# Chunked attention and two feed-forward layers: the PSUM scratch of the second layer as one tile of two banks, or as two tiles of one bank

## The chip, the cores and the metric

One core of one Trainium2 chip runs the whole kernel. The metric is the device time of an execution in microseconds (us); the figure for a kernel is the median of its timed runs.

## The reference

Three stages follow each other on 2304 tokens (4 x 576) of 512 features. The first is attention inside chunks of 64 tokens, for 8 heads of 64 features. The other two are feed-forward layers with 2048 hidden features, without residuals:

```python
# layer 1
h = x @ w_in;  g = softplus(h);  x = g @ w_out
# layer 2
h = x @ w_in
P = a[0] + a[1]*h + a[2]*h*h + a[3]*h*h*h
Q = 1 + abs(b[0])*abs(h) + abs(b[1])*h*h
g = P / (Q + 1e-6)
out = g @ w_out
```

The output is float32, 2304 x 512.

## The kernel before

The tokens are cut into five blocks (512, 512, 512, 384 and 384; `BLOCKS`), and the hidden features into 16 slices of 128. A **step** is one slice of one block: 80 steps in layer 1, then 80 in layer 2, numbered on by `s`. In layer 2 the blocks come in the order 512, 384, 384, 512, 512 (`ORDER2`).

A float32 operand is split into two parts, and each product is made of three products of parts. So a step of layer 2 has

- `products_h` (matmuls at L726): 12 matmuls over the tokens of the block into one PSUM bank `h` (pool `ps_h`, two buffers of one bank);
- `rational` (from L779 on), the function above on `h`, by ScalarE (ACT) and VectorE (DVE);
- `products_out2` (L915): three matmuls of 512 columns for each 128 tokens of the block, so 12 or 9, into PSUM tiles `acc` of two banks (pool `ps_acc`, two buffers). They take the upper part of `g` from ACT (L823) and the lower part from GpSimd (POOL, L826).

At the end of a block `evacuate` copies each `acc` tile to SBUF, its first bank by ACT (L948), its second by DVE (L950), and SyncE stores it.

In `rational` a scratch area `u` in PSUM holds one value after the other. In the order in which a step adds them, its operations are:

| engine, line | in the profile | what |
|---|---|---|
| ACT L793 (`square`) | `u<-h` | u = h*h |
| ACT L811 (`linear`) | `t<-h,b_t` | d = abs(b0*h) |
| ACT L841 | `t<-h,na_t` | p = -(a3*h + a2) |
| DVE L796 | `t<-u,absb_t,t` | d = abs(b1)*u + d |
| DVE L852 | `t<-h,t` | p = h*p |
| DVE L796 | `t<-t,na_t,h` | p = (p - a1)*h |
| ACT L815 (`log`) | `u<-t,epsq_t` | u = ln(d + const) |
| ACT L819 (`exp`) | `u<-u` | u = exp(-u), a first reciprocal |
| DVE L796 | `t<-t,epsq_t,u` | d = (d + const)*u |
| DVE L796 | `u<-t,na_t,u` | u = (p - a0)*u |
| DVE L796 | `t<-t,u` | p = (d - 2)*u |
| ACT L823 (`hi`) | `g<-t` | upper part of g |
| POOL L826 (`lo`) | `g<-t,g` | lower part of g |

All DVE operations built by the helper `stt` have L796 as their line; they are told apart by their operands. d and p are SBUF tiles, both named t in the profile.

PSUM is full: `ps_acc` four banks, `ps_h` two, `ps_att` two. `ps_att` holds one tile of [128, 2, 512] float32, used by the attention during layer 1. In layer 2 it is `u`, allocated once in `square` of the first step: even steps use the half [:, 0], odd steps [:, 1].

The order of the work is written out beforehand. `Program` collects every operation as a task with an engine, a cost and the names of what it reads and writes, and `schedule` plans a start for each by its costs; the tasks are then issued in the order of those starts, so each engine works through a fixed list. For the planner the halves of `u` are two things (`ku, kp = ("att", s % 2), turn("t2", 3)`). The waits between engines are not the planner's: the framework below derives them from the tiles which each instruction reads and writes, in the order of issue.

Of the kernel before, what the change touches and what calls it, by code (L numbers as in the profile page):

```python
# [11 lines left out]
F32 = mybir.dt.float32  # L12
# [5 lines left out]
PSUM = bass.MemoryType.PSUM  # L18
DRAM = bass.MemoryType.DRAM

P = 128
# [21 lines left out]
class Program:  # L43
# [24 lines left out]
    def add(self, engine, cost, fn, reads=(), writes=(), alloc=None, after=(), table=None):  # L68


        i = len(self.tasks)
        deps = {}
        before = list(after)
        for key in reads:
            before += [self.writer[key]]
            self.readers.setdefault(key, []).append(i)
        for key in writes:
            if key in self.writer:
                before.append(self.writer[key])
            before += self.readers.pop(key, [])  # L80
            self.writer[key] = i
        for j in before:
            if j != i:
                deps[j] = self.tasks[j][1] + self.delay(self.tasks[j][0], engine)
        if alloc is not None:
            if alloc in self.last_alloc:
                deps.setdefault(self.last_alloc[alloc], 0.0)
            self.last_alloc[alloc] = i
        self.tasks.append((engine, cost, fn))
        self.deps.append(deps)  # L90
        self.table.append(table)
        return i
# [97 lines left out]
def tile_chunk_attention_two_ffn(  # L190
# [43 lines left out]
    dpool = ctx.enter_context(tc.tile_pool(name="dpool", bufs=1, space=DRAM))  # L234
    ps_acc = ctx.enter_context(tc.tile_pool(name="ps_acc", bufs=2, space=PSUM))
    ps_h = ctx.enter_context(tc.tile_pool(name="ps_h", bufs=2, space=PSUM))
    ps_att = ctx.enter_context(tc.tile_pool(name="ps_att", bufs=1, space=PSUM))

    ident = const.tile([P, P], F32, name="ident")
    epsq_t = const.tile([P, 1], F32, name="epsq_t")  # L240
# [12 lines left out]
    def table(name):  # L253

        if loaded[0] != name:
            loaded[0] = name
            act.preload_act_table_set(name)

    def on_act(n, pointers=0):
        return 0.05 + 0.095 * pointers + n / 1200  # L260

    def on_dve(n, pointers=0):
        return 0.07 + 0.06 * pointers + n / 960

    def turn(tag, bufs):

        counts[tag] = counts.get(tag, -1) + 1
        return tag, counts[tag] % bufs
# [6 lines left out]
    x = {}  # L275
# [461 lines left out]
    def scratch(s, n_tok, third=False):  # L737
        t = {}

        def new(tag):  # L740
            if tag == "t1" and third:
                tile = att1.tile([P, T], F32, tag="v", name=f"{tag}_{s}")
            else:
                tile = (tmp if tag == "t1" else tmp3).tile([P, T], F32, tag=tag, name=f"{tag}_{s}")
            t[tag] = tile[:, :n_tok]
            return t[tag]

        return t, new

    def new_g(s, third=False):  # L750
        p, tag = (att1, "qkT") if third else (gpool, "g")
        gs[s] = p.tile([P, 2, T], F32R, tag=tag, name=f"g_{s}")
# [26 lines left out]
    def rational(s, hkey, j, start):  # L779
        n_tok = BLOCKS[j][1]  # L780
        third = s % 3 == 2
        t, new = scratch(s, n_tok, third)
        ku, kp = ("att", s % 2), turn("t2", 3)
        kd, kg = ((("v", 0)), "g third") if third else (turn("t1", 2), turn("g", 2))
        old = [("turned", "later", n) for n in range(16)] if third else []

        def u():
            return x["u"][:, s % 2, :n_tok]

        def square():  # L790
            if start:
                x["u"] = ps_att.tile([P, 2, 512], F32, tag="att", name="u")
            act.activation(u(), h(), AF.Square)  # L793

        def stt(out, in0, scalar, in1, op0, op1):
            return lambda: vec.scalar_tensor_tensor(  # L796
                out=out(), in0=in0(), scalar=scalar, in1=in1(), op0=op0, op1=op1
            )

        def h():  # L800
            return hs[s]

        def d():
            return t["t1"]

        def p():
            return t["t2"]

        def linear():
            table(EXP_LN)  # L810
            act.activation(new("t1"), h(), AF.Abs, scale=b_t[:, 0:1])  # L811

        def log():
            table(EXP_LN)
            act.activation(u(), d(), AF.Ln, bias=epsq_t)  # L815

        def exp():
            table(EXP_LN)
            act.activation(u(), u(), AF.Exp, scale=-1.0)  # L819

        def hi():
            new_g(s, third)
            act.activation(gs[s][:, 0, :n_tok], p(), AF.Copy)  # L823

        def lo():
            pool.tensor_tensor(  # L826
                out=gs[s][:, 1, :n_tok], in0=p(), in1=gs[s][:, 0, :n_tok].bitcast(F32),
                op=ALU.subtract,
            )

        add(
            ACT, on_act(n_tok), square, [hkey], [("att", 0), ("att", 1)] if start else [ku],
            alloc="att" if start else None,
        )
        add(
            ACT, on_act(n_tok, 1), linear, [hkey, "b"], [kd], alloc="v" if third else "t1",
            table=EXP_LN,
        )
        add(
            ACT, on_act(n_tok, 2),  # L840
            lambda: act.activation(  # L841
                new("t2"), h(), AF.Identity, scale=na_t[:, 3:4], bias=na_t[:, 2:3]
            ),
            [hkey, "na"], [kp], alloc="t2",
        )
        add(
            DVE, on_dve(n_tok, 1), stt(d, u, absb_t[:, 1:2], d, ALU.mult, ALU.add),
            [ku, kd, "absb"], [kd],
        )
        add(  # L850
            DVE, on_dve(n_tok),
            lambda: vec.tensor_tensor(out=p(), in0=h(), in1=p(), op=ALU.mult), [hkey, kp], [kp],  # L852
        )
        add(
            DVE, on_dve(n_tok, 1), stt(p, p, na_t[:, 1:2], h, ALU.add, ALU.mult), [hkey, kp], [kp]
        )
        add(ACT, on_act(n_tok, 1), log, [kd], [ku], table=EXP_LN)
        add(ACT, on_act(n_tok), exp, [ku], [ku], table=EXP_LN)
        add(DVE, on_dve(n_tok, 1), stt(d, d, epsq_t, u, ALU.add, ALU.mult), [kd, ku], [kd])
        add(DVE, on_dve(n_tok, 1), stt(u, p, na_t[:, 0:1], u, ALU.add, ALU.mult), [kp, ku], [ku])  # L860
        add(DVE, on_dve(n_tok), stt(p, d, 2.0, u, ALU.subtract, ALU.mult), [ku, kd], [kp])
        add(
            ACT, on_act(n_tok), hi, [kp], [(kg, 0), *old], alloc="qkT" if third else "g"
        )
        add(POOL, 0.2 + n_tok / 430, lo, [kp, (kg, 0)], [(kg, 1)])
        return kg
# [158 lines left out]
    s = -1  # L1025
# [130 lines left out]
```

## Time and profile before

| what | value |
|---|---|
| median of 3 runs | 907.72 us (906.89 to 907.83) |
| profiled execution | 905.86 us, its span 904.1 us |
| mean granted clock of TensorE | 0.997 |
| busy share of the span: PE, PEld, DVE, ACT, POOL | 95%, 80%, 72%, 57%, 29% |
| layer 2 on TensorE | first matmul at 452.97 us; its last 66 matmuls in a row begin at 883.22 us |
| DMA over the span, mean | 79 GB/s |

PE is TensorE's matmuls, PEld its weight loads. A line of the timeline has the start, the duration, the engine, the line of code, the operation with its operands and shapes, and how many alike follow each other; in brackets stands how long the engine was idle before and on whom it waited. The duration of a row runs from start to result, and back-to-back instructions overlap a little, so a pace is read from starts.

### The profile page before, as it was taken

Reading aid. Unit: us, or ns where it says so; the run is one execution under the profiler, and the core shown is the slowest. Engines: PE = TensorE matmul, PEld = TensorE weight load, DVE = VectorE, ACT = ScalarE, POOL = GpSimd, SP = SyncE. Lnnn points to the kernel's source line nnn. Section 1 sums busy time; section 2 is a strip of 40 time slices with the busy share of each in tenths; the row PEclk is TensorE's granted clock in tenths of the full one; section 3 lists DMA queues with packets and bytes.
Section 4 is the critical chain, followed back from the end, with each engine's and each line's share of the span. In section 5 each row is a group of like instructions: output and inputs, shape, how many; then the busy total and the mean of one; then the engine's idle time right before and its main releaser. Section 6 shows DMA issues by size and latency. Waiting matters only on the chain.

```text
span 904.1 us, 13291 instructions
## 1 busy us (share of the span) xinstructions
PE 862.1 (95%) x5068; PEld 726.1 (80%) x5068; DVE 649.2 (72%) x1102; ACT 511.2 (57%) x864; POOL 258.4 (29%) x238
## 2 busy tenths in 40 slices
PE   8999999999999999999989999999898999999977
PEld 7777889999997788888767778788787777778755
DVE  4788787828999888169746677677677776777764
ACT  4899962233334333354477566666766756667653
POOL 0132332221222221253537122421432242212212
PEclk9999999999999999999999999999999999999999
DMA  9784525025444333265412001200000200000001
GB/s 213 200 227 154 187 71 106 12 59 163 117 106 140 105 109 108 70 217 162 129 46 95 0 1 29 100 1 1 36 1 1 82 1 1 0 33 15 1 0 47
DMA packets 76928, 71.11 MB, mean 79 GB/s; under 512 B 36160, under 2 KB 63808, under 8 KB 76864
## 3 DMA queue, kind: packets, MB, share of 16 engines
q1 hardware_dynamic: 76864, 70.27, 27.1%
q8 instruction: 39, 0.64, 0.3%
q14 instruction: 25, 0.20, 0.1%
HBM read 56.63 MB, written 13.63 MB: 78 GB/s over the span
## 4 chain that ended last, share of the span: by engine, by line
DVE 36%; PE 36%; ACT 20%; issue 6%; POOL 1%; DMA 1%; ACTq 0%; DVEq 0%; SPq 0%; POOLq 0%
DVE t L796 18%; PE h L726 16%; PE acc L885 14%; DVE u L796 6%; ACT u L793 5%; ACT u L815 4%; DVE t L852 3%; ACT u L819 3%; ACT t L811 2%; ACT g L823 2%; DVE qkT L520 2%; ACT t L841 2%; PE aps L541 1%; DVE cm_2o L361 1%; DVE cm_2i L361 1%
## 5 line engine op out<-in xcount | busy, mean ns | idle before, releaser
L915 PE MATMUL acc<-w_2o,g 128*128 128x512 f32 x864 | 216.9, 395 | 19.2 <-POOL g L826 11.4
L726 PE MATMUL h<-xT,w_2i 128*128 128x512 f32 (+1 forms) x960 | 212.9, 372 | 11.1 <-DVE t L796 9.5
L726 PE MATMUL h<-xT,w_1i 128*128 128x512 f32 (+1 forms) x960 | 211.3, 370 | 3.1 <-ACT g L766 1.6
L885 PE MATMUL acc<-g,w_1o 128*128 128x512 f32 (+1 forms) x960 | 211.7, 370 | 0.0
L915 PEld LDWEIGHTS acc<-w_2o,g 128*128 128x128 f32 x864 | 159.5, 188 | 64.0 <-POOL g L826 20.9
L726 PEld LDWEIGHTS h<-xT,w_2i 128*128 128x128 f32 x960 | 175.9, 189 | 41.4 <-DVE t L796 14.3
L726 PEld LDWEIGHTS h<-xT,w_1i 128*128 128x128 f32 x960 | 173.6, 188 | 27.5 <-ACT g L766 2.5
L885 PEld LDWEIGHTS acc<-g,w_1o 128*128 128x128 f32 x960 | 173.8, 188 | 23.0
L826 POOL TENSOR_TENSOR g<-t,g 128x512 fp32r<-128x512 f32 (+1 forms) x80 | 94.4, 1180 | 299.9 <-ACT g L823 192.0
L769 POOL TENSOR_TENSOR g<-t,g 128x512 fp32r<-128x512 f32 (+1 forms) x80 | 98.2, 1228 | 238.5 <-ACT g L766 221.7
L761 ACT ACTIVATE t<-h 128x512 f32<-128x512 f32 (+1 forms) x80 | 44.2, 553 | 94.8 <-PE h L726 94.7
L796 DVE SCALAR_TENSOR_TENSOR t<-u,absb_t,t 128x512 f32<-128x512 f32 (+1 forms) x80 | 55.6, 695 | 46.1 <-ACT u L793 22.7
L766 ACT ACTIVATE g<-h 128x512 fp32r<-128x512 f32 (+1 forms) x80 | 44.3, 554 | 63.6 <-PE acc L885 63.0
L520 DVE STREAM_TRANSPOSE qkT<-qk 32x256 f32<-32x256 f32 x176 | 76.9, 437 | 3.0
L796 DVE SCALAR_TENSOR_TENSOR t<-t,epsq_t,u 128x512 f32<-128x512 f32 (+1 forms) x80 | 55.4, 692 | 30.2 <-ACT u L819 25.4
L815 ACT ACTIVATE u<-t,epsq_t 128x512 f32<-128x512 f32 (+1 forms) x80 | 52.0, 650 | 43.3 <-DVE t L796 32.3
L823 ACT ACTIVATE g<-t 128x512 fp32r<-128x512 f32 (+1 forms) x80 | 46.8, 585 | 49.3 <-DVE t L796 47.1
L793 ACT ACTIVATE u<-h 128x512 f32<-128x512 f32 (+1 forms) x80 | 43.2, 540 | 47.3 <-DVE t L796 24.7
L852 DVE TENSOR_TENSOR t<-h,t 128x512 f32<-128x512 f32 (+1 forms) x80 | 50.8, 634 | 24.7 <-ACT t L811 17.8
L796 DVE SCALAR_TENSOR_TENSOR u<-t,na_t,u 128x512 f32<-128x512 f32 (+1 forms) x80 | 55.8, 698 | 10.9 <-ACT u L793 8.1
L796 DVE SCALAR_TENSOR_TENSOR t<-t,na_t,h 128x512 f32<-128x512 f32 (+1 forms) x80 | 55.4, 692 | 8.7 <-ACT u L793 3.7
L796 DVE SCALAR_TENSOR_TENSOR t<-t,u 128x512 f32<-128x512 f32 (+1 forms) x80 | 50.6, 632 | 12.5 <-ACT u L793 6.4
(79 smaller groups left out, 764.0 us busy)
## 6 DMA issues: line engine op xcount, KB each, us to landing
wr_1i<-in_moe_w_in_dram SPq DMA_DIRECT2D x16, 512.0 KB, 3.9
wr_1o<-in_moe_w_out_dram SPq DMA_DIRECT2D x16, 512.0 KB, 4.7
wr_2i<-in_moe_w_in_dram SPq DMA_DIRECT2D x16, 512.0 KB, 3.9
wr_2o<-in_moe_w_out_dram SPq DMA_DIRECT2D x16, 512.0 KB, 4.5
out_dram<-ev SPq DMA_DIRECT2D x18, 256.0 KB, 2.0
qk<-in_q_dram SPq DMA_DIRECT2D x16, 256.0 KB, 5.1
qk<-in_k_dram SPq DMA_DIRECT2D x16, 256.0 KB, 5.3
v<-in_v_dram SPq DMA_DIRECT2D x16, 256.0 KB, 4.6
```

The lines of the kernel that those rows point to most:

```text
L520: vec.transpose(tiles["qkT"][p0 : p0 + 32, n, :, c * CH : (c + 1) * CH].rearrange("p g (u t) -> p g t u", t=2), qk_t[tb][p1 : p1 + 32, h:: ...
L726: pe.matmul(hs[s], w[:, a, c * P : (c + 1) * P], xt[:, b, c, :n_tok], start=n == 0, stop=n == 3 * KC - 1,)
L766: act.activation(gs[s][:, 0, :n_tok], hs[s], AF.Softplus)
L769: pool.tensor_tensor(out=gs[s][:, 1, :n_tok], in0=t["t2"], in1=gs[s][:, 0, :n_tok].bitcast(F32), op=ALU.subtract,)
L793: act.activation(u(), h(), AF.Square)
L796: return lambda: vec.scalar_tensor_tensor(out=out(), in0=in0(), scalar=scalar, in1=in1(), op0=op0, op1=op1)
L815: act.activation(u(), d(), AF.Ln, bias=epsq_t)
L823: act.activation(gs[s][:, 0, :n_tok], p(), AF.Copy)
L826: pool.tensor_tensor(out=gs[s][:, 1, :n_tok], in0=p(), in1=gs[s][:, 0, :n_tok].bitcast(F32), op=ALU.subtract,)
L852: lambda: vec.tensor_tensor(out=p(), in0=h(), in1=p(), op=ALU.mult), [hkey, kp], [kp],
L885: pe.matmul(accs[1, j, half][:, c % 2, :n_tok], wts[1, "o", fc][:, a, c * P : (c + 1) * P], gs[s][:, b, :n_tok], start=first and n == 0, s ...
L915: pe.matmul(accs[2, j, half][:, c % 2], gs[s][:, b, c * P : (c + 1) * P], wts[2, "o", fc][:, a, :], start=first and n == 0, stop=last and ...
```

## The change

The pool `ps_att` goes into an exit stack of its own. In `square` of the first step of layer 2 that pool is closed, a new pool `ps_u` is opened, and two tiles of [128, 512] float32 are allocated in it, one bank each, with tags of their own. Even steps use the one and odd steps the other. Operations, their operands' sizes, the tasks, their costs, names and order stay as they were.

```diff
     ps_h = ctx.enter_context(tc.tile_pool(name="ps_h", bufs=2, space=PSUM))
-    ps_att = ctx.enter_context(tc.tile_pool(name="ps_att", bufs=1, space=PSUM))
+    att_stack = ctx.enter_context(ExitStack())
+    ps_att = att_stack.enter_context(tc.tile_pool(name="ps_att", bufs=1, space=PSUM))
...
         def u():
-            return x["u"][:, s % 2, :n_tok]
+            return x["u", s % 2][:, :n_tok]
 
         def square():
             if start:
-                x["u"] = ps_att.tile([P, 2, 512], F32, tag="att", name="u")
+                att_stack.close()
+                ps_u = ctx.enter_context(tc.tile_pool(name="ps_u", bufs=1, space=PSUM))
+                for n in range(2):
+                    x["u", n] = ps_u.tile([P, 512], F32, tag=f"u{n}", name=f"u{n}")
             act.activation(u(), h(), AF.Square)
```

## Rows read from the trace of the kernel before

**Rows 1.** The page: busy us of each engine, share of span, instructions

```profile
PE 862.1 (95%) x5068; PEld 726.1 (80%) x5068; DVE 649.2 (72%) x1102; ACT 511.2 (57%) x864; POOL 258.4 (29%) x238
```

**Rows 2.** Groups by form, PE, 473.3 to 883.2: busy, mean ns, idle before

```profile
L915 PE MATMUL acc<-w_2o,g 128*128 128x512 f32 x798 | 201.1, 395 | 19.0 <-POOL g L826 11.4 <-ACT g L823 3.8 <-DVE ev L950 3.7
L726 PE MATMUL h<-xT,w_2i 128*128 128x512 f32 x528 | 128.5, 394 | 6.4 <-DVE t L796 6.4
L726 PE MATMUL h<-xT,w_2i 128*128 128x384 f32 x384 | 72.6, 338 | 2.8 <-DVE t L796 2.2 <-ACT u L793 0.5
```

**Rows 3.** Timeline, PE in layer 2: start, us, instruction [idle before, releaser]

```profile
473.31 3.01 PE L915 MATMUL acc<-w_2o,g 128*128 128x512 f32 x12 [1.23 <-DVE ev L950]
...
620.40 4.35 PE L726 MATMUL h<-xT,w_2i 128*128 128x384 f32 x24
624.59 1.08 PE L915 MATMUL acc<-w_2o,g 128*128 128x512 f32 x4
...
788.60 5.60 PE L726 MATMUL h<-xT,w_2i 128*128 128x512 f32 x24
794.04 5.60 PE L915 MATMUL acc<-w_2o,g 128*128 128x512 f32 x24
...
872.70 3.01 PE L726 MATMUL h<-xT,w_2i 128*128 128x512 f32 x12 [1.13 <-DVE t L796]
879.01 4.37 PE L726 MATMUL h<-xT,w_2i 128*128 128x512 f32 x12 [3.30 <-DVE t L796]
883.22 15.93 PE L915 MATMUL acc<-w_2o,g 128*128 128x512 f32 x66
```

**Rows 4.** Chain of waits that ended last, 473.3 to 883.2, by line

```profile
by line: DVE t L796 38.8%; DVE u L796 11.9%; ACT u L793 9.6%; ACT u L815 7.2%; DVE t L852 6.8%; ACT u L819 5.6%; ACT g L823 5.3%; ACT t L811 5.1%; issue 5.0%; ACT t L841 3.2%; DVE ev L950 1.1%; ACT ev L948 0.2%; ACTq L823 0.1%; ACTq L793 0.
```

**Rows 5.** Timeline, ACT and DVE, one step of a 384-token block

```profile
583.21 0.47 ACT L793 ACTIVATE u<-h 128x384 f32<-128x384 f32 x1 [0.21 <-DVE t L852]
...
583.72 0.62 DVE L796 SCALAR_TENSOR_TENSOR u<-t,na_t,u 128x384 f32<-128x384 f32 x1 [0.54 <-ACT u L793]
...
584.38 0.62 DVE L796 SCALAR_TENSOR_TENSOR t<-u,absb_t,t 128x384 f32<-128x384 f32 x1
584.91 0.54 DVE L796 SCALAR_TENSOR_TENSOR t<-t,u 128x384 f32<-128x384 f32 x1
...
585.49 0.58 ACT L815 ACTIVATE u<-t,epsq_t 128x384 f32<-128x384 f32 x1 [1.80 <-DVE t L796]
...
587.63 0.47 ACT L793 ACTIVATE u<-h 128x384 f32<-128x384 f32 x1 [0.74 <-DVE t L796]
```

**Rows 6.** Waits, 473.3 to 883.2: us in total, times, longest us

```profile
ACT u L793 <- DVE u L796: 12.0, 12, 1.5
...
DVE u L796 <- ACT u L793: 7.5, 12, 0.7
ACT u L793 <- DVE t L852: 7.4, 10, 1.5
...
DVE t L852 <- ACT t L811: 6.0, 5, 2.1
...
DVE t L852 <- ACT u L793: 5.3, 6, 2.0
ACT t L811 <- DVE t L852: 4.4, 7, 0.8
...
PE acc L915 <- DVE ev L950: 3.7, 3, 1.6
```

**Rows 7.** Timeline, ACT and DVE near the end

```profile
873.47 0.58 ACT L819 ACTIVATE u<-u 128x512 f32<-128x512 f32 x1 [0.76 <-DVE t L796]
...
876.76 0.76 DVE L796 SCALAR_TENSOR_TENSOR u<-t,na_t,u 128x512 f32<-128x512 f32 x1 [0.65 <-ACT u L793]
```

**Rows 8.** Timeline, the beginning of layer 2

```profile
455.82 4.24 PE L885 MATMUL acc<-g,w_1o 128*128 128x512 f32 x18
456.02 0.58 ACT L793 ACTIVATE u<-h 128x512 f32<-128x512 f32 x1 [2.58 <-PE h L726]
```

## The prediction

> **What bounds the kernel now.** I read the page first. PE is busy for 862 us of a span of 904.1 us [rows 1], so the kernel looks bound by its matmuls, with little left to win. The groups by form of the stretch from 473.3 to 883.2, which is layer 2 without its first steps and its last matmuls, put a size on that little: the idle times before the three groups of matmuls are 19.0, 6.4 and 2.8 us, 28.2 in all [rows 2].
>
> Busy rows of matmuls overlap and their ends are modelled, so I measure the same stretch by starts. At full pace 24 matmuls of 512 columns take 794.04 - 788.60 = 5.44 us, 0.2267 each, and 24 of 384 columns 624.59 - 620.40 = 4.19 us, 0.1746 each [rows 3]. The stretch has 798 + 528 matmuls of 512 and 384 of 384 [rows 2]: 300.6 + 67.0 = 367.6 us at that pace. It lasts from the first group of outputs at 473.31 to the last 66 at 883.22 [rows 3], 409.9 us. So **TensorE loses 42.3 us**, about half a microsecond in each step.
>
> The Trainium skill ("Trainium Kernel Development and Optimization", Performance Expectations) calls matmul busy time a bad metric because matmuls are pipelined. The rows agree: by busy time the loss would be 28.2 us, by starts it is 42.3. I use the second, and by the first everything below would shrink by a third.
>
> Who makes TensorE wait? The chain of waits says it plainly: in the same stretch it hardly ever goes through PE. ACT and DVE hold nearly all of it, alternating [rows 4]. So although PE is busy 95% of the time, the end is set by a chain of ACT and DVE operations that is a little slower than TensorE's pace.
>
> One step shows why that chain is so long [rows 5]. Call the step whose square is at 583.21 B, the one before A and the one after C. (1) DVE's `u<-t,na_t,u` at 583.72 belongs to A, whose scratch is the other half of `u`; still it waits 0.54 us, till B's square has ended at 583.68. (2) B's logarithm (L815) needs d, which `t<-u,absb_t,t` finishes at 584.38 + 0.62 = 585.00. It starts at 585.49, just behind A's `t<-t,u`, which ends at 585.45: 0.45 us too late. (3) C's square waits 0.74 us till 587.6, though it only reads `h` and writes the half that B does not use. All three couple an odd step to an even one. They are as they would be if the two halves counted as one thing, so that in the order of issue every write of either half and every use of the other queue up. From B's square to C's takes 4.42 us; TensorE needs 12 x 0.1746 + 9 x 0.2267 = 4.14 us for such a step. The chain is the longer one.
>
> The list of waits has more of that kind: ACT's square behind DVE's `u` operation 12.0 us in 12 waits, and the reverse 7.5 us in 12 [rows 6]. The step's own square and `u` operation are far apart, so these pairs belong to different steps.
>
> **The change, part by part.** No instruction is added, removed or resized, and the planner gets the same tasks with the same costs, so every engine keeps its list and order; SP's and POOL's queues are passed by nothing. Closing one pool and opening another costs nothing as long as the first square, at 456.02 [rows 8], waits only for the attention's last read of the old tile, work that belongs to layer 1 and lies far ahead. What changes is that the halves become separate tiles, so the waits between even and odd steps go.
>
> *A step in the middle.* Without the three waits, B to C takes 4.42 - 0.54 - 0.45 - 0.74 = 2.69 us. That is 1.45 below TensorE's 4.14. TensorE is late next: it becomes the bound, and the chain runs ahead until it waits for `h`.
>
> *What remains of the 42.3 us.* Three terms.
> - Waits on the bank of `h`. DVE and ACT also wait for each other when they read the same `h`: the rows L793 behind L852, L852 behind L811, L852 behind L793 and L811 behind L852 have 7.4 + 6.0 + 5.3 + 4.4 = 23.1 us in 28 waits [rows 6]. The change leaves these. On average one is 0.8 us, which fits into the 1.45 us that a step gains, but several in a row do not. Bounds: 0 if all are covered, 23.1 if none is. I take a third, 7.7, nearer to zero because of that comparison.
> - Evacuations at the ends of blocks: PE waits 3.7 us for L950 [rows 6]. The copies are late because they stand in the lists of ACT and DVE behind late work, and the two of a tile still follow each other. Bounds 0 and 3.7; I take half, 1.9.
> - The end. From 872.70 to 883.22, 10.52 us, PE runs 24 matmuls worth 5.44 us [rows 3]: 5.1 lost. In the period from 872.70 to 879.01 two cross-step waits stand, 0.76 and 0.65 us [rows 7]. Without them 6.31 becomes 4.90, and TensorE, which has 2.72 us to do there, still loses 2.2. The 12 matmuls behind that pause take 4.21 us till the next group instead of 2.72; I leave that 1.5 as it is. So 3.7 of 5.1 stays. Bounds: 3.7 and 5.1, as the gain here may also be swallowed.
>
> Kept: 7.7 + 1.9 + 3.7 = 13.3 us. **Gain: 42.3 - 13.3 = 29.0 us.** Nothing is counted for the steps before 473.3, nor for the 66 last matmuls and the stores, which run at pace. The profiled execution took 905.86 us, so it becomes 876.9. That execution lies 1.86 us below the median 907.72, so the forecast of the median is **878.7 us**.
>
> Bounds of the forecast: with nothing kept but the 3.7 of the end, the gain is 38.6 and the median 869.1; with all three terms at their upper bounds (23.1 + 3.7 + 5.1 = 31.9), the gain is 10.4 and the median 897.3.
>
> **The rivals.**
>
> *The bank of `h` takes over (22%).* Each step reads `h` three times by ACT and twice by DVE. If the planner's order, which does not know of waits between readers, puts these reads in alternation, the 23.1 us of waits stay on the path in full: gain 42.3 - 23.1 = 19.2, median **888.5**. For it: such a wait opens the very step worked out above (0.21 behind L852 at 583.21) [rows 5]. Against it: 1.45 us of new slack in a step.
> The Trainium skill ("PSUM — Partial Sum Buffer", PSUM bank collisions raise a hardware error) says that two engines have to be kept apart on one bank in the same 32 partitions, reads against reads included, while accesses to different banks run clean side by side. The waits between readers of `h` agree with the first half; by that rule they stay after the change and 888.5 is the mark, whereas the waits between the halves of `u`, different banks, are not needed.
>
> *Nothing changes (5%).* The two new tiles could be ordered just as the halves were, or every wait that goes could be followed at once by another of the same length: **907.7**. Against it: in rows 5 each of the three waits has nothing else behind it that ends as late.
>
> *Slower: the pool, not the tile, is what is ordered (3%).* If the framework holds tiles of one pool together, the halves stay coupled, and the first square must in addition wait for what was issued before the new pool is opened. Place: 456.02, with 18 matmuls of layer 1 just begun at 455.82 [rows 8]. They run till 455.82 + 18 x 0.2267 = 459.9, so the square and all behind it are 3.9 us later: **911.6**. It decides from the point where the boundary costs more than the uncoupling gives, so only if that gives under 3.9 us. Against it: `h` tiles of one pool must be independent for PE to run ahead of ACT, as it does now.
>
> **How the numbers follow.** The forecast, TensorE bound again, has 70%; its own range is 869 to 884. The `h` rival has 22%, from 884 to 897. No change has 5%, slower 3%. To leave out no more than 2 in 10, I let the range go from the lower bound, 869, to **893**, past the middle of the `h` rival. What a measurement can tell from no change here is 0.2%, 1.8 us. Faster by more than that: 0.92. Within: 0.05. Slower: 0.03.
>
> **What would show it.** Right: PE's loss by starts over layer 2 falls from 42 us to some 13; the chain of waits runs mainly through PE; the rows L793 behind DVE u and DVE u behind L793 disappear; a 384-token step takes 4.1 to 4.2 us from square to square, set by `h`. The waits between L793, L811 and L852 are still there. The `h` rival: these rows grow and the chain stays on ACT and DVE, through L852. No change: rows 5 and 6 come back as they are. Slower: the first square later than at 456.0. The prediction is wrong if the cross-step waits are gone and PE still loses over 25 us, or if they are not gone.

## The result, and the profile after

The changed kernel takes 867.40 us (866.55 to 868.92, four runs), the kernel before 907.31 us in the same comparison. The ratio is 0.9564, with a 95% interval of 0.9547 to 0.9581: 39.9 us faster. The forecast was 878.7 us with a range from 869 to 893. The direction came true, and so did the part of the mechanism that concerns the change; the time lies 1.6 us below the range, and the gain was forecast at 29.0 us.

The page after, busy time of each engine:

```profile
PE 849.2 (98%) x5068; PEld 728.5 (84%) x5068; DVE 644.6 (74%) x1102; ACT 508.1 (59%) x864; POOL 258.1 (30%) x238
```

The groups by form on PE, from the first outputs of layer 2 to its last 66 matmuls, which answer to [rows 2]:

```profile
L919 PE MATMUL acc<-w_2o,g 128*128 128x512 f32 x798 | 192.6, 390 | 0.3 <-DVE ev L954 0.3
L727 PE MATMUL h<-xT,w_2i 128*128 128x512 f32 x528 | 126.6, 390 | 2.2 <-DVE t L800 2.2
L727 PE MATMUL h<-xT,w_2i 128*128 128x384 f32 x384 | 71.3, 336 | 0.0
```

The idle time before these matmuls fell from 28.2 to 2.5 us; waits for `g` (POOL, ACT) are gone altogether. The first and last group of that stretch, and the end:

```profile
472.98 3.01 PE L919 MATMUL acc<-w_2o,g 128*128 128x512 f32 x12 [0.29 <-DVE ev L954]
...
837.43 3.01 PE L727 MATMUL h<-xT,w_2i 128*128 128x512 f32 x12 [0.38 <-DVE t L800]
842.23 3.06 PE L727 MATMUL h<-xT,w_2i 128*128 128x512 f32 x12 [1.78 <-DVE t L800]
845.12 15.29 PE L919 MATMUL acc<-w_2o,g 128*128 128x512 f32 x66
```

By starts: 845.12 - 472.98 = 372.1 us against 367.6 at full pace, so TensorE loses **4.5 us where it lost 42.3**. Of the 38.7 us by which the span became shorter (904.1 to 865.4), 37.8 come from here.

The chain of waits in the same stretch, beside [rows 4]:

```profile
by line: PE h L727 45.2%; PE acc L919 44.6%; DVE t L800 3.4%; DVE t L856 1.3%; DVE u L800 1.1%; ACT u L819 0.9%; issue 0.9%; ACT t L815 0.9%; ACT t L845 0.8%; ACT u L823 0.5%; ACT u L797 0.5%; DVE ev L954 0.2%; DVEq L856 0.0%; ACT g L827 0.
```

It now runs through TensorE for 90%. (Lines have moved: the matmuls' L726 is L727 and L915 is L919; ACT's L793 is L797, L811 is L815, the logarithm L815 is L819, the exponential L819 is L823, L841 is L845; on DVE L852 is L856 and L796 is L800.) Of the waits in [rows 6], these are left:

```profile
ACT u L797 <- DVE t L856: 7.5, 10, 1.6
DVE t L856 <- ACT t L815: 6.8, 8, 2.3
...
ACT t L815 <- DVE t L856: 4.6, 7, 1.0
DVE t L856 <- ACT u L797: 4.3, 5, 2.0
```

The two rows of the cross-step waits, the square behind the `u` operation (12.0 us) and the reverse (7.5 us), don't occur any more. A larger row, which the prediction did not list, has nearly gone with them: the square behind DVE's other operations at L796, 24.7 us in 24 waits before and 1.8 us in 3 now. The third wait of the worked step is one of these. The listed waits on the bank of `h` are what they were: 7.5 + 6.8 + 4.6 + 4.3 = 23.2 us in 30 waits, before 23.1 in 28. The list leaves out DVE's second read of `h`, whose line is that of the helper: idle time of 8.5 us stood before it, and 9.2 us now, mostly behind ACT's reads of `h`.

### The profile page after: what moved, and what is told of

Read it like the earlier page. It is cut to its first block, busy times and chain, and to the rows that moved or that the text cites. A ratio compares the mean times of both kernels' runs of the same rounds, so it can differ in the third digit from the quotient of the medians.

```text
span 865.4 us, 13261 instructions
## 1 busy us (share of the span) xinstructions
PE 849.2 (98%) x5068; PEld 728.5 (84%) x5068; DVE 644.6 (74%) x1102; ACT 508.1 (59%) x864; POOL 258.1 (30%) x238
## 4 chain that ended last, share of the span: by engine, by line
PE 78%; DVE 11%; ACT 4%; issue 4%; POOL 1%; DMA 1%; SPq 0%; DVEq 0%; POOLq 0%; ACTq 0%
PE h L727 37%; PE acc L919 21%; PE acc L889 15%; DVE qkT L521 2%; DVE t L800 2%; PE aps L542 1%; DVE cm_2o L362 1%; DVE cm_2i L362 1%; DVE aT L615 1%; PE aps L631 1%; PE warm L1116 1%; DVE t L856 1%; PE aps L496 1%; ACT t L815 1%; POOL w_2o L292 1%
## 5 line engine op out<-in xcount | busy, mean ns | idle before, releaser
L727 PE MATMUL h<-xT,w_1i 128*128 128x512 f32 (+1 forms) x960 | 211.3, 370 | 3.1 <-ACT g L767 1.6
L727 PE MATMUL h<-xT,w_2i 128*128 128x512 f32 (+1 forms) x960 | 209.8, 369 | 4.1 <-DVE t L800 3.0
L919 PE MATMUL acc<-w_2o,g 128*128 128x512 f32 x864 | 207.9, 390 | 0.3 <-DVE ev L954 0.3
L727 PEld LDWEIGHTS h<-xT,w_2i 128*128 128x128 f32 x960 | 175.6, 188 | 30.7 <-DVE t L800 4.7
L727 PEld LDWEIGHTS h<-xT,w_1i 128*128 128x128 f32 x960 | 173.6, 188 | 27.5 <-ACT g L767 2.5
L919 PEld LDWEIGHTS acc<-w_2o,g 128*128 128x128 f32 x864 | 161.6, 188 | 33.7 <-DVE ev L954 1.0
L800 DVE SCALAR_TENSOR_TENSOR t<-u,absb_t,t 128x512 f32<-128x512 f32 (+1 forms) x80 | 55.6, 695 | 42.1 <-ACT u L797 21.2
L856 DVE TENSOR_TENSOR t<-h,t 128x512 f32<-128x512 f32 (+1 forms) x80 | 50.8, 635 | 25.8 <-ACT t L815 19.1
L800 DVE SCALAR_TENSOR_TENSOR t<-t,epsq_t,u 128x512 f32<-128x512 f32 (+1 forms) x80 | 55.4, 692 | 18.6 <-ACT u L823 17.5
L819 ACT ACTIVATE u<-t,epsq_t 128x512 f32<-128x512 f32 (+1 forms) x80 | 52.1, 651 | 25.1 <-DVE t L800 22.6
L815 ACT ACTIVATE t<-h,b_t 128x512 f32<-128x512 f32 (+1 forms) x80 | 51.2, 640 | 20.4 <-PE h L727 15.2
L800 DVE SCALAR_TENSOR_TENSOR t<-t,na_t,h 128x512 f32<-128x512 f32 (+1 forms) x80 | 55.4, 692 | 9.4 <-ACT t L815 4.1
L845 ACT ACTIVATE t<-h,na_t 128x512 f32<-128x512 f32 (+1 forms) x80 | 58.5, 731 | 4.6 <-PE h L727 4.6
L797 ACT ACTIVATE u<-h 128x512 f32<-128x512 f32 (+1 forms) x80 | 43.2, 541 | 21.6 <-PE h L727 12.2
```

Source lines behind the costliest of these rows:

```text
L727: pe.matmul(hs[s], w[:, a, c * P : (c + 1) * P], xt[:, b, c, :n_tok], start=n == 0, stop=n == 3 * KC - 1,)
L800: return lambda: vec.scalar_tensor_tensor(out=out(), in0=in0(), scalar=scalar, in1=in1(), op0=op0, op1=op1)
L845: lambda: act.activation(new("t2"), h(), AF.Identity, scale=na_t[:, 3:4], bias=na_t[:, 2:3]),
L919: pe.matmul(accs[2, j, half][:, c % 2], gs[s][:, b, c * P : (c + 1) * P], wts[2, "o", fc][:, a, :], start=first and n == 0, stop=last and ...
```

## Experiments

The theory: the halves of one tile tied even steps to odd ones, and that made the chain of ACT and DVE longer than TensorE's pace. Rivals: the new pool by itself; the waits on the bank of `h`; losses of TensorE from elsewhere. The table has the loss of TensorE by starts, worked out as above, from the first outputs of layer 2 and the first of its last outputs in the timeline of each run. In the runs with ordered reads (before_rf, pad_rf, reads_first_again) the last outputs in a row are 60 and not 66, so 804 matmuls of outputs lie before them instead of 798, and 369.0 us is the full pace there instead of 367.6.

| run | median us | first outputs | last outputs | TensorE loses |
|---|---|---|---|---|
| before | 907.3 | 473.31 | 883.22 | 42.3 |
| changed | 867.4 | 472.98 | 845.12 | 4.5 |
| square_sbuf | 885.1 | 474.10 | 861.25 | 19.6 |
| before_act_no_h | 890.3 | 473.02 | 865.94 | 25.3 |
| before_rf | 889.2 | 473.94 | 865.84 | 22.9 |
| pad_before | 950.8 | 475.64 | 926.30 | 83.1 |
| pad_after | 892.4 | 473.92 | 869.21 | 27.7 |
| pad_act_no_h | 880.3 | 473.68 | 857.24 | 16.0 |
| pad_rf | 869.7 | 472.57 | 846.96 | 5.4 |
| reads_first_again | 863.4 | 472.52 | 842.62 | 1.1 |

### The pool, or the tiles? (pool_only)

```diff
-                for n in range(2):
-                    x["u", n] = ps_u.tile([P, 512], F32, tag=f"u{n}", name=f"u{n}")
+                both = ps_u.tile([P, 2, 512], F32, tag="u", name="u")
+                for n in range(2):
+                    x["u", n] = both[:, n]
```

> The old pool is closed and a new one opened as in the change, but the new pool holds one tile of two banks with the halves for even and odd steps, as before. Theory (the two tiles do it, by taking away the waits between even and odd steps): no gain, 906 to 909 us, ACT's square behind DVE's u operation again some 12 us in 12 waits. Rival (it is the new pool: other addresses, or another release of the old tile): the time of the changed kernel, 866 to 869 us.

906.74 us, ratio 0.9999 (0.9988 to 1.001). In its list of waits, over the stretch of [rows 6]:

```profile
ACT u L798 <- DVE u L801: 12.0, 12, 1.5
...
DVE u L801 <- ACT u L798: 7.5, 12, 0.7
```

The same two rows to the digit. The new pool gives nothing; separate tiles do.

### The square alone (square_sbuf, on the kernel before)

```diff
-            act.activation(u(), h(), AF.Square)
+            x["sq", s] = cvt.tile([P, 512], F32, tag="m", name=f"sq_{s}")
+            act.activation(sq(), h(), AF.Square)
...
-            stt(d, u, absb_t[:, 1:2], d, ALU.mult, ALU.add),
+            stt(d, sq, absb_t[:, 1:2], d, ALU.mult, ALU.add),
```

> The kernel before with one tile of two banks, but the square is written to a tile in SBUF, so that u is touched only from the logarithm on. Of the three cross-step waits of the worked step the first (0.54) and the third (0.74) go, the second (0.45, the logarithm behind the other step's last product) stays. Theory: a 384-token step falls from 4.42 to 3.14 us, under the 4.14 that TensorE needs, so most of the gain comes from the square alone: 869 to 882 us. Rival (only the whole separation helps, since the logarithm and the u operation still follow each other through the steps): 895 us or more.

885.06 us, ratio 0.976 (0.9732 to 0.9788): between the two marks, and a miss for both. Without the square's coupling 21.7 us come back, somewhat over half of the gain. The edit has a price of its own, though: DVE's operation on the square now has both operands in SBUF, and over its 80 steps it is busy for 66.5 us instead of 55.6.

```profile
L800 DVE SCALAR_TENSOR_TENSOR t<-sq,absb_t,t 128x512 f32<-128x512 f32 (+1 forms) x80 | 66.5, 832 | 34.1 <-ACT sq L797 17.7
```

If all of these 10.9 us lay on the chain, the coupling would be worth up to 32.6 us, an estimate; the run does not tell how much of them does. What remains shows in the waits:

```profile
ACT u L819 <- DVE t L800: 37.6, 50, 2.2
...
ACT u L819 <- DVE u L800: 7.7, 5, 2.1
```

Both are waits of the logarithm. The second row is that behind the `u` operation of another step, 8.7 us in 5 waits before. In the changed kernel it is gone, and the first row has 20.7 us in 29 waits (30.3 in 31 before the change).

### How much slack has the chain? (pad_before, pad_after)

```diff
             act.activation(u(), u(), AF.Exp, scale=-1.0)
+            act.activation(u(), u(), AF.Copy)
```

> The kernel before with one more ACT copy of u onto itself behind the exponential of each step, unknown to the planner, so the order stays. Each lengthens the chain of its step by about 0.62 us (512 tokens) or 0.51 us (384): 48 x 0.62 + 32 x 0.51 = 46 us if the chain of ACT and DVE is the bound all through. Theory: 935 to 955 us. Rival (TensorE was the bound and its losses came from elsewhere): under 915 us.

> The changed kernel with the same extra ACT copy in each step. Theory (TensorE is the bound, with over a microsecond of slack in a step): 867 to 875 us, PE losing under 12 us in layer 2. Rival (the waits on the bank of h have become the chain that sets the end): 890 us or more, since the same 46 us then lie on the path.

In the kernel before the copy costs 950.79 - 906.73 = 44.1 us. That is all that it adds to the chain, estimated at 46 and by its rows in the trace (0.58 and 0.48 us) 43: ACT and DVE were the bound all through. The chain of waits of pad_before from the first to the last outputs goes through PE for under 4%. In the changed kernel it costs 892.41 - 867.40 = 25.0 us. That is the rival's mark (890 us or more) and a miss for the theory. But less than the full length came through: some 19 us were hidden, on average a quarter of a microsecond in each of 80 steps, not the 1.45 us that the worked step had promised. The bound is back on ACT and DVE, as the chain of waits of pad_after over layer 2 says:

```profile
by line: DVE t L800 29.8%; ACT u L819 10.9%; DVE u L800 9.8%; ACT u L823 9.2%; ACT u L824 9.1%; ACT g L828 6.3%; ACT t L815 5.4%; issue 5.2%; ACT u L797 4.8%; ACT t L846 3.6%; DVE t L857 3.4%; ACT ev L953 0.8%; DVE ev L955 0.6%; DMA out_dra
```

Why is the slack so small? The same squares as in [rows 5], B, C and now D behind them, on ACT in the changed kernel:

```profile
572.62 0.47 ACT L797 ACTIVATE u<-h 128x384 f32<-128x384 f32 x1 [0.43 <-DVE t L856]
...
575.14 0.44 ACT L797 ACTIVATE u<-h 128x384 f32<-128x384 f32 x1
...
580.92 0.47 ACT L797 ACTIVATE u<-h 128x384 f32<-128x384 f32 x1
```

and D in the kernel before, with what stands ahead of it on ACT:

```profile
592.87 0.53 ACT L823 ACTIVATE g<-t 128x384 fp32r<-128x384 f32 x1 [1.86 <-DVE t L796]
593.30 0.47 ACT L793 ACTIVATE u<-h 128x384 f32<-128x384 f32 x1
```

From B to C it now takes 2.52 us (forecast 2.69, before 4.42). But from C to D it takes 5.78 us, as it did before (593.30 - 587.63 = 5.67): in ACT's fixed list D's square stands behind the upper part of C's `g`, so that step runs through nearly its whole chain. Steps come in a short and a long one here. The pair took 10.09 us before and takes 8.30 now, without a wait of ACT or DVE for TensorE in it; TensorE needs 2 x 4.14 = 8.28. The worked step was the short one.

### Are the waits on the bank of h on the chain?

First try, DVE's side (before_no_h, after_no_h, pad_after_no_h):

```diff
+        def other():
+            return wts[2, "i", (s - 80) % FC][:, 0, :n_tok].bitcast(F32)
...
-            lambda: vec.tensor_tensor(out=p(), in0=h(), in1=p(), op=ALU.mult), [hkey, kp], [kp],
+            lambda: vec.tensor_tensor(out=p(), in0=other(), in1=p(), op=ALU.mult), [hkey, kp], [kp],
...
-            DVE, on_dve(n_tok, 1), stt(p, p, na_t[:, 1:2], h, ALU.add, ALU.mult), [hkey, kp], [kp]
+            DVE, on_dve(n_tok, 1), stt(p, p, na_t[:, 1:2], other, ALU.add, ALU.mult), [hkey, kp], [kp]
```

> The kernel before, but DVE's two operations on h read a weight tile in SBUF instead (the polynomial comes out of other numbers; sizes and order stay). So DVE and ACT no longer wait for each other on the bank of h. Theory (the cross-step waits on u made the chain too long): the chain keeps them and gets shorter only where an h wait stood on it, so TensorE still loses over 25 us: 890 to 906 us. Rival (the 23 us of h waits were what mattered, together with anything that shortens the chain by as much): under 886 us.

> The same replacement in the changed kernel. TensorE loses 4.5 us there between the first outputs and the last 66 matmuls, 2.8 of it at the end, behind DVE's reads of h. Theory (the h waits are covered but for the end): 862 to 867 us. Rival (they still hold back more than that): under 862 us, which the loss left in the trace has no room for.

> The changed kernel with the extra ACT copy in each step (892.4 us with DVE reading h) and with DVE's reads of h replaced by a weight tile. If the h waits are what uses up the slack that the worked step promised, the copy is hidden again: 866 to 875 us. If the slack is used up by DVE's own list and the true dependencies of a step, the time stays at 885 to 893 us.

909.18, 865.52 and 892.32 us. The first lies outside both of its ranges; the others lie in the theory's range and in that of DVE's own list. None of the three can settle what the waits cost, because the replacement made DVE slower. Of before_no_h, by form:

```profile
L796 DVE SCALAR_TENSOR_TENSOR t<-t,na_t,w_2i 128x512 f32<-128x512 f32 x43 | 45.4, 1056 | 1.2
L855 DVE TENSOR_TENSOR t<-w_2i,t 128x512 f32<-128x512 f32 x43 | 32.7, 760 | 4.8 <-ACT t L844 4.7
```

The kernel before has 746 and 687 ns there: with both operands in SBUF the two together are on average 0.38 us longer in a step of 512 tokens, and 0.31 in one of 384. That makes some 28 us over 80 steps, about as much as the waits that the replacement takes away (23 us listed, 8.5 not).

Second try, ACT's side, with the order kept (before_act_no_h, and pad_act_no_h with the extra copy):

```diff
-            act.activation(u(), h(), AF.Square)
+            act.activation(u(), other(), AF.Square)
...
-            act.activation(new("t1"), h(), AF.Abs, scale=b_t[:, 0:1])
+            act.activation(new("t1"), other(), AF.Abs, scale=b_t[:, 0:1])
```

> The kernel before, in its own order, but ACT's square and its absolute value read a weight tile in SBUF in place of h (other numbers, same sizes). Only the third ACT read of h is left, which DVE's reads have to follow anyway, so hardly a wait on the bank of h remains, and the order of the lists is that of before. If the h waits were part of the chain that bound the kernel: 880 to 895 us, near the 889 us of the kernel before with ordered reads. If only the cross-step waits were: 902 to 908 us.

> The same replacement in the changed kernel with the extra ACT copy in each step (892.4 us), order kept. If the h waits use up the slack of a step: 867 to 876 us, as with ordered reads (869.7 us). If it was some other thing in the new order that gave the slack back: 885 to 893 us.

890.33 us, ratio 0.9815 (0.9787 to 0.9844): with the cross-step waits still there (the square behind the `u` operation has 11.8 us in 13 waits, the reverse 6.3 in 12), 16.7 us come back. So the h waits were on the chain as well. The replacement also spares ACT its waits for TensorE's `h`, but of those the kernel before has only 1.8 us. With the copy the changed kernel falls from 892.4 to 880.3 us, between the two marks and about half of the way: the h waits use up a part of the slack.

Third, the h reads ordered by the planner (reads_first; before_rf and pad_rf have the same edit on the kernel before and on pad_after):

```diff
-        add(
+        reads = [add(
             ACT, on_act(n_tok), square, [hkey], [("att", 0), ("att", 1)] if start else [ku],
...
-        add(
+        reads += [add(
             ACT, on_act(n_tok, 1), linear, [hkey, "b"], [kd], alloc="v" if third else "t1",
...
             lambda: vec.tensor_tensor(out=p(), in0=h(), in1=p(), op=ALU.mult), [hkey, kp], [kp],
+            after=reads,
```

> The changed kernel, with the planner told that DVE's first read of h follows all three of ACT's, so that no ACT read of h waits for DVE; the order of the list changes accordingly. If the h waits cost the 2.8 us at the end and little else: 863 to 867 us. If holding DVE back costs more than the alternation: 868 us or more.

> The same instruction to the planner in the kernel before, with one tile of two banks. If the h waits had a share in the 42 us that TensorE lost there, ordering the reads gives a good part of their 23 us back: 885 to 898 us. If the cross-step waits set the chain's length alone, the gain stays small: 900 to 908 us.

> The changed kernel with the extra ACT copy in each step (892.4 us) and with DVE's reads of h planned behind ACT's. If the alternation of the h reads is what uses up the slack of a step: 868 to 880 us. If it is the length of the step's own operations on ACT and DVE: 887 to 894 us.

On the kernel before: 889.22 us, 17.7 less, nearly the same as without the h waits. This order changes other waits too: the square behind the `u` operation has 18.2 us in 18 waits there, 12.0 in 12 before. With the extra copy: 869.70 us, against 892.4; of the copy's length most is hidden again. On the changed kernel: 863.35 us, ratio 0.9523 (0.9507 to 0.9539). That beats both kernels, so it was run once more beside the changed one:

> The changed kernel once more, as the mark for the next run: 866 to 869 us.

> DVE's first read of h planned behind ACT's reads, as in the run reads_first (863.4 us), now beside the changed kernel with more rounds. If its gain is real: 862.5 to 865 us, 2 to 5 us under the changed kernel, the intervals apart. If it was scatter: within 1 us of it.

869.19 us, ratio 0.9571 (0.9558 to 0.9584), and 863.44 us, ratio 0.9519 (0.9506 to 0.9532). The mark missed by a little, but the intervals are apart; ordering the reads is worth 4 to 6 us on top of the change. TensorE loses 1.1 us there.

That pad_rf gives back more (22.7 us) than pad_act_no_h (12.1) has a part that was not taken apart. ACT's two operations that read SBUF there are a little longer (the absolute value on 512 tokens 714 against 683 ns), and the planned order differs in more than the h reads; which of them it is stays open.

## Why the prediction was right and where it was wrong

**Right: what bounds the kernel.** The copy that costs its full length before the change shows it: TensorE was busy 95% of the span, and the chain of ACT and DVE set the end. The loss of 42.3 us by starts was the right measure of what could be won; the 28.2 us of idle time are less than the 37.8 that were gained in that stretch.

**Right: what the change removes.** The cross-step rows are gone, the pool by itself does nothing, and the worked step came out at 2.52 us for 2.69.

**Wrong: the waits on the bank of `h`, kept at 7.7 us.** This is the step that failed, a term of the sum that was sized too large. The waits themselves remained in full, 23.2 us in 30. The rule of the Trainium skill ("PSUM — Partial Sum Buffer", PSUM bank collisions raise a hardware error), that two engines are to be kept apart on one bank, reads against reads included, agrees with that. But they cost TensorE next to nothing: of the 4.5 us that it loses, 845.12 - 837.43 - 5.44 = 2.25 belong to the end, and 2.3 are left in all the rest of the stretch, whatever their cause, where 7.7 + 1.9 had been kept for these waits and the evacuations. The term put waits of ACT and DVE down as time that TensorE loses. They are that only while the chain of ACT and DVE is the bound, and the same prediction had TensorE as the bound; after the change the chain of waits runs through TensorE for 90%.

**Wrong: the reason for taking a third.** It compared a mean wait of 0.8 us with a slack of 1.45 us in a step. The worked step was the short one of a pair; over that pair the chain has no slack, and on average a step has a quarter of a microsecond. The h waits fit all the same, since the chain including them was on average just shorter than TensorE's pace. The forecast was right that TensorE is the bound again, but the 1.45 us on which it rested this are not there. That only the cross-step waits made the chain too long before the change is wrong as well: without the h waits, or with ordered reads, the kernel before gains 17 us. Each of the two kinds of wait lengthened the chain; with the cross-step ones gone, ordering the reads wins 4 to 6 us.

**Wrong by less: evacuations and the end.** Of 3.7 us for the evacuations 0.3 is left, where 1.9 was kept. That 0.3 stands before the first row of the stretch, as 1.23 of the 3.7 did, so it isn't a part of the 4.5. The end was kept at 3.7 us and costs 2.25; its last period, forecast at 4.90 us, is 842.23 - 837.43 = 4.80. The 1.5 us of slow matmuls behind the long pause did not come, and that was luck. They are a matter of TensorE's granted clock: in the kernel before it is 0.52 from 880 to 882 us, the lower level of 1.2 GHz, behind a pause of 3.30 us. The changed kernel's profile has 1.00 at that place, from 842 to 846 us. The same kernel run again (after_again) has the same pause of 1.78 us, but a clock of 0.50 from 844 to 846 us:

```profile
842.27 4.60 PE L727 MATMUL h<-xT,w_2i 128*128 128x512 f32 x12 [1.78 <-DVE t L800]
846.72 3.58 PE L919 MATMUL acc<-w_2o,g 128*128 128x512 f32 x15
```

There the 12 matmuls take 4.45 us till the next group instead of 2.89, and TensorE loses 846.72 - 473.04 - 367.6 = 6.1 us in the stretch instead of 4.5.

**Why the time fell below the range.** The median lies 11.3 us under the forecast. Of that, 8.8 are the stretch of layer 2, where 37.8 us were gained instead of 29.0: 7.3 by the waits on `h` and the evacuations, 1.5 by the end. A further 0.9 was won outside of the stretch, where nothing had been counted. The last 1.7 have nothing to do with the change: the profiled execution of the kernel before lay 1.86 us below the median, and the forecast added this again, but that of the changed kernel lies only 0.17 below its median. By the stretch alone the gain stays inside the stated bounds (10.4 to 38.6); the two other parts carry the time past the lower end of 869.

**The rivals.** The `h` rival's 888.5 did not come, since the 23 us are not on the path once the chain is shorter than the pace. But in the kernel before a good part of them was (16.7 us came back without them), and with half a microsecond more in each step they are again about half of what the copy costs: its mechanism was right, its moment was not. No change and a slower kernel are refuted by the result, and a cost of the new pool by pool_only.

## What to carry to other kernels

Where steps alternate between halves of one PSUM tile, look in the waits for pairs of instructions that share no data; separate tiles took no more space here and were worth 4.4%, with TensorE 95% busy. To find out whether a chain of other engines is the bound and how much slack it has, lengthen it by a known amount: the copy told more than any replay of a step. When a step is replayed by hand, replay as many as repeat, since a fixed order can come in short and long steps, and don't put the waits of other engines down as TensorE's loss when TensorE is to be the bound.

## What the runs showed of the hardware that was not expected

That DVE gets slower with both operands in SBUF is no fixed price. In the timeline of before_no_h, DVE's product with the weight tile stands beside POOL's work:

```profile
770.09 1.29 POOL L829 TENSOR_TENSOR g<-t,g 128x512 fp32r<-128x512 f32 x1 [2.11 <-ACT g L826]
770.64 1.28 DVE L855 TENSOR_TENSOR t<-w_2i,t 128x512 f32<-128x512 f32 x1 [1.43 <-ACT t L844]
```

Issued at 770.64, while POOL subtracts from 770.09 to 771.38, it takes 1.28 us: it ends 0.54 us behind POOL. Of its rows on 512 tokens in layer 2, those that no row of POOL overlaps take 0.68 to 0.69 us, as with `h` in PSUM; all that take longer, up to 1.51, overlap one. The form with a scalar pointer has 0.74 to 0.75 us without POOL beside it and up to 1.80 with it. The Trainium skill ("SBUF — State Buffer", Who interferes with whom) says that a DVE instruction with two SBUF inputs contends with a GpSimd instruction that reads SBUF; the rows agree. It is why a replacement operand has to lie in the same memory, or the experiment measures something else.
